# Attention followed by a gated unit on one core: the first queries in two halves, bfloat16 constants, 37 weight steps on GpSimd, a new order of work for block 0

## The chip, the cores and the metric

The kernel runs on one core of a Trainium2 chip. A core has five engines with queues of their own, which run beside each other and meet through semaphores: TensorE (PE, its weight loads shown as PEld), VectorE (DVE), ScalarE (ACT), GpSimd (POOL) and SyncE (SP), whose queue issues nearly all DMAs. The metric is the device time of one execution in microseconds (us).

## The reference

Eight batches (called blocks here) of 576 tokens pass through attention with eight heads of 64 columns; four heads see a local window of 32 keys, four see every 32nd key. What comes out, 4608 tokens of 512 columns, goes through a gated unit with 1536 hidden columns.

```python
scores = scale * np.matmul(q, k.transpose(0, 1, 3, 2))
mask_local = (rel >= 0) & (rel < 32)
mask_strided = (rel >= 0) & (pos[None, :] % 32 == pos[:, None] % 32)
scores = np.where(masks, scores, -1e9)
attn = np.exp(scores - np.max(scores, axis=-1, keepdims=True))
attn = attn / (np.sum(attn, axis=-1, keepdims=True) + 1e-09)
x = np.matmul(attn, v)            # heads side by side: 4608 x 512
gate = 1.0 / (1.0 + np.exp(-(x @ w_gate)))
out = (gate * (x @ w_val)) @ w_out
```

## The kernel before

**The large products.** Each float32 operand is split into a high and a low part that TensorE multiplies at its rate for rounded values, and a product is made of three matmuls (high by high, high by low, low by high; line 550 for gate and value, line 581 for the output). There are 12 slices f of the hidden columns; slice f needs three weights, f.0 (gate), f.1 (value), f.2 (output), and there are 36 in all. Later blocks are taken two at a time with a scheme of sums and differences (line 816).

**A weight's way.** A weight comes from memory as 64-bit words (`wr`, line 231, SP). ACT makes two words of it (`wa` line 252, `wb` line 256), DVE shifts one (`ws`, line 260) and adds the two as integers (`wd`, line 264, which DVE does with an instruction of its own on 16-bit halves), ACT rounds the sum to the high part (`wu`, line 268), and DVE subtracts that from the sum for the low part (`wl`, line 271). `whole` and `lower`, the functions behind `wd` and `wl`, already take the engine as an argument.

**Attention by pairs.** A block has four pairs of heads: 0 and 2 are local, 1 and 3 strided. For pair p of block b the steps are: loads `fQb.p` and `fVb.p`; scores `fS` (line 349, and for block 0 the mask, added by matmuls with a bfloat16 identity and mask, line 360); `fA` the row maximum (line 383), `fU` its subtraction (line 393), `fE` the exponential on ACT (line 408), `fN` the row sum (lines 412 to 414: sum, plus 1e-9, reciprocal), `fWp` the row multiplication on POOL (line 418; `fW` is the same on DVE); then a transposition, in block 0 on PE (`fT`, lines 426 and 430; ACT copies it out in `fP`, lines 447 and 449), later on DVE (`fB`, line 439); `fX` the product with v (line 471); and `fH` (ACT, line 507), `fL` (DVE, line 511) and `fR` (ACT, line 520), which split the result into the rows of x. In the text S0.3 is the score step of block 0, pair 3, and so for T, X, A, U and the others.

**Products of block 0.** As x of block 0 comes pair by pair, the products of the first slices are cut in four: `fgf.i.c` is the part of weight f.i with one 128-row chunk of x (three matmuls); `fgf.i` is a whole one (twelve). `of` is the output product of slice f (twelve); `s`, `m`, `x`, `y` are the sigmoid, the gating and the split of the hidden values.

**Order.** All steps are written out in one long list, `ORDER`; each engine does its share in the order of that list, and a DMA queue is an engine in this sense. Which PSUM bank a step uses is in `BANKS` (default `a`; X0.0 has o1, X0.1 o0, T0.0 and T0.1 share a, T0.2 o0). A step that uses a bank waits until what was there before has been read.

**Constants.** `cst` (float32: local mask, strided mask, identity; line 871) and `half` (bfloat16, the strided mask repeated; line 874) are two loads.

**The end.** `glu_out` for the last group makes the four row tiles in the order 0, 2, 1, 3. `give_out` (line 597) copies a finished tile from PSUM and stores it with two DMAs (line 603); tile 3 is copied in two halves of columns, first by ACT, then by DVE, and each engine's half is stored with two DMAs by one queue, ACT's by ACT and DVE's by SP.

Of the kernel before, what the change touches and what calls it, by code (L numbers as in the profile page):

```python
# [20 lines left out]
DM, DF = 512, 1536  # L21
# [41 lines left out]
    "X0.0": "o1", "S0.1": "o1", "X0.1": "o0", "S0.2": "o0", "T0.2": "o0", "X0.2": "o0", "S0.3": "o1", "T0.3": "o0", "X0.3": "o1", "g1": "a",  # L63
# [12 lines left out]
fQ0.0 fZ0.1 fZ0.3 K fQ0.1 C fQ0.2 fV0.1 fQ0.3 wr0.1 wr0.0 fV0.0 fV0.3 fV0.2 fS0.0 wr1.1 wr1.0 wr0.2 fS0.1 fA0.0 fQ1.0 wr2.0 wr2.1 fU0.0 wr1.2 fE0.0  # L76
fA0.1 fS0.2 fN0.0 fU0.1 fWp0.0 fA0.2 fE0.1 fS0.3 fU0.2 fN0.1 fE0.2 fT0.0 wb0.1 fN0.2 fWp0.1 fP0.0 wb0.0 fA0.3 wa0.1 fWp0.2 fT0.1 fU0.3 wa0.0 wr3.0
wr2.2 ws0.1 fX0.0 fP0.1 wd0.1 fE0.3 ws0.0 fX0.1 fN0.3 fH0.0 fV1.0 fR0.0 wu0.1 wd0.0 fWp0.3 fH0.1 fR0.1 fL0.1 wu0.0 wa1.1 fL0.0 fT0.2 wb1.1 wl0.0 wb1.0
wr3.2 ws1.1 fg0.0.0 wd1.1 fP0.2 wl0.1 wu1.1 fg0.0.1 wa1.0 wl1.1 fT0.3 wa0.2 wr3.1 ws1.0 wb0.2 wd1.0 fg0.1.0 fP0.3 ws0.2 wr4.0 fS1.0 wd0.2 wu1.0 wl1.0
wu0.2 fX0.2 wa2.0 fM1.0 fQ1.1 wb2.0 ws2.0 fA1.0 wr4.1 fX0.3 fH0.2 wa2.1 fL0.2 fR0.2 wd2.0 fg1.0.0 fH0.3 ws2.1 wu2.0 fg0.1.1 fL0.3 wb2.1 fg0.0.2 wl2.0  # L80
wa1.2 wr4.2 fg0.1.2 fU1.0 wb1.2 fg1.1.0 wd2.1 wr5.0 fE1.0 fg0.0.3 ws1.2 wu2.1 fN1.0 fg1.0.1 fg1.1.1 wl2.1 fg1.0.2 s0.0 fW1.0 wa2.2 fg1.1.2 wd1.2 wb3.0
fg0.1.3 wl0.2 wu1.2 fg2.0.0 m0.0 fR0.3 fg1.1.3 fB1.0.0 x0.0 fg2.0.1 wa3.1 y0.0 wa3.0 fg2.1.0 wl1.2 wb3.1 fg1.0.3 wr5.2 fB1.0.2 wr6.0 o0.0 s0.1 wa4.0
m0.1 fB1.0.1 x0.1 wb4.0 y0.1 wb2.2 fg2.1.1 wr6.2 ws3.0 wa4.1 wr5.1 fS1.1 fB1.0.3 wb3.2 wb4.1 wd3.0 fZ1.1 fg2.0.2 fQ1.2 fM1.1 wu3.0 wr7.0 fg2.1.2 wa3.2
# [36 lines left out]
c3.0.1.6 y3.0 V3.0.5 e2.3 B12.3 d2.3 G3.0.7 r8 B12.0 V3.0.7 Z13 c3.0.0.7 ad3.0.0.7 G3.0.4 c3.0.1.7 sg3.0.7 ad3.0.1.7 V3.0.4 sg3.0.4 mu3.0.7 G3.0.3 r9  # L120
# [54 lines left out]
y8.11 ob8  # L175
"""
FEW, MOST = slice(0, BY_PE), slice(BY_PE, B)
NEG = -1.0e30
SCALE = 1.0 / D**0.5


@with_exitstack
def attention_then_glu(ctx, tc, qk_l, qk_s, v_l, v_s, w_all, consts, halves, out):
# [689 lines left out]
    def half_constants():  # L873
        nc.sync.dma_start(half, halves)
# [124 lines left out]
```

## Time and profile before

| | us |
|---|---|
| median of three runs | 936.56 |
| the three runs | 935.67, 936.56, 936.94 |
| the profiled execution | 936.08 |
| its span, first to last instruction | 934.2 |
| PE busy | 916.7 (98%) |
| PE weight loads | 755.3 (81%) |
| DVE busy | 614.2 (66%) |
| ACT busy | 428.7 (46%) |
| POOL busy | 125.9 (13%) |

The profile is of one execution. Times in its rows count from the start of the span. A timeline row gives the start, the duration, the engine, the line, the operation, the tiles written and read, and in brackets the idle time of the engine before it and what ended that. A row of a group gives the total, then the mean in ns, then the idle time before. Matmuls are pipelined, so the duration of one is longer than the distance to the next.

### The profile page before, as it was taken

What the parts mean: (1) busy time and instruction counts of PE and PEld (TensorE: products, weight loads), DVE (VectorE), ACT (ScalarE), POOL (GpSimd) and SP (SyncE); (2) the same over time, 40 slices, a digit from 0 to 9 for tenths busy, and PEclk for the clock granted to TensorE, in tenths of its full rate; (3) what the DMA queues carried; (4) which work ended last, traced back from release to release, by engine and by line L of the source; (5) the groups of instructions that cost most, each with busy time, mean ns of one, the idle gap of its engine ahead of it and who ended that gap; (6) DMA issues with size and microseconds to landing.
All of it is one profiled execution on the core that took longest, in us unless ns stands there. A gap on an engine that the chain in (4) does not pass through costs nothing.

```text
span 934.2 us, 18488 instructions
## 1 busy us (share of the span) xinstructions
PE 916.7 (98%) x7608; PEld 755.3 (81%) x7608; DVE 614.2 (66%) x1013; ACT 428.7 (46%) x775; POOL 125.9 (13%) x186
## 2 busy tenths in 40 slices
PE   6799999999999999999999999999999999999998
PEld 4688888888888888888888888888888888888886
DVE  5799996667689989766667897766347343333331
ACT  3789764334455455444445444444435233332231
POOL 2000003545415623000000120000003000000000
PEclk9999999999999999999999999999999999999999
DMA  9862535554556675656555425654444055444111
GB/s 352 307 230 89 185 96 174 176 175 154 179 190 190 216 222 199 215 191 188 173 190 177 149 99 175 207 189 143 145 141 144 12 168 187 143 156 140 64 45 46
DMA packets 90212, 154.60 MB, mean 166 GB/s; under 512 B 5904, under 2 KB 40336, under 8 KB 90128
## 3 DMA queue, kind: packets, MB, share of 16 engines
q1 hardware_dynamic: 89648, 152.77, 50.4%
q8 instruction: 60, 0.98, 0.4%
q10 hardware_dynamic: 480, 0.66, 0.3%
q14 instruction: 24, 0.20, 0.1%
HBM read 121.94 MB, written 31.46 MB: 164 GB/s over the span
## 4 chain that ended last, share of the span: by engine, by line
PE 98%; DMA 1%; issue 0%; DVE 0%; ACT 0%; SPq 0%
PE o L581 22%; PE p L816 21%; PE d L816 16%; PE g L550 10%; PE v L550 10%; PE o_a L581 5%; PE o_g L581 3%; PE o_v L581 3%; PE x_a L471 2%; PE x L471 1%; PE s_v L349 1%; PE s_g L349 1%; PE s L349 1%; DMA qk<-in_qk_s 1%; PE gv L550 1%; PE t L426 1%
## 5 line engine op out<-in xcount | busy, mean ns | idle before, releaser
L816 PE MATMUL p<-xs,ring 128*128 128x512 f32 x864 | 204.6, 389 | 0.0
L816 PEld LDWEIGHTS p<-xs,ring 128*128 128x128 f32 x864 | 162.2, 188 | 33.6
L581 PE MATMUL o<-w,hh 128*128 128x512 f32 x576 | 180.7, 395 | 0.0
L816 PE MATMUL d<-xs,ring 128*128 128x512 f32 x648 | 155.7, 389 | 0.0
L816 PEld LDWEIGHTS d<-xs,ring 128*128 128x128 f32 x648 | 121.7, 188 | 25.2
L581 PEld LDWEIGHTS o<-w,hh 128*128 128x128 f32 x576 | 106.1, 188 | 22.7
L439 DVE STREAM_TRANSPOSE pt<-sb 32x320 f32<-32x320 f32 (+1 forms) x224 | 120.0, 536 | 4.2
L581 PE MATMUL o<-w,hl 128*128 128x512 f32 x288 | 112.1, 389 | 0.0
L850 DVE TENSOR_TENSOR e<-e,d 128x512 f32<-128x512 f32 x54 | 37.1, 688 | 108.1 <-PE d L816 62.1
L550 PE MATMUL g<-xh,w 128*128 128x512 f32 x256 | 86.3, 395 | 0.0
L550 PE MATMUL v<-xh,w 128*128 128x512 f32 x256 | 85.8, 392 | 0.0
L845 ACT COPY e<-p 128x512 f32<-128x512 f32 x54 | 31.8, 588 | 116.6 <-PE p L816 116.4
L581 PEld LDWEIGHTS o<-w,hl 128*128 128x128 f32 x288 | 54.1, 188 | 11.5
L550 PEld LDWEIGHTS g<-xh,w 128*128 128x128 f32 x256 | 48.7, 190 | 10.5 <-issue 0.2
L550 PEld LDWEIGHTS v<-xh,w 128*128 128x128 f32 x256 | 48.5, 189 | 10.1
L744 POOL TENSOR_TENSOR sum<-sum 128x128 f32<-128x128 f32 x96 | 51.9, 543 | 6.5
L574 DVE TENSOR_TENSOR hl<-hid,hh 128x512 fp32r<-128x512 f32 x36 | 28.0, 780 | 34.0 <-ACT hh L570 33.8
L550 PE MATMUL g<-xl,w 128*128 128x512 f32 x128 | 50.3, 393 | 0.0
L550 PE MATMUL v<-xl,w 128*128 128x512 f32 x128 | 50.1, 391 | 0.0
L739 POOL TENSOR_TENSOR sum<-w 128x256 f32<-128x256 f32 x44 | 34.7, 809 | 98.8 <-DMA sets<-sum 71.3
L858 ACT ACTIVATE e<-e 128x512 f32<-128x512 f32 x54 | 34.2, 634 | 27.9 <-DVE e L850 27.6
L570 ACT CAST hh<-hid 128x512 fp32r<-128x512 f32 x36 | 22.5, 624 | 49.5 <-PE o_a L581 41.1
(149 smaller groups left out, 1373.7 us busy)
## 6 DMA issues: line engine op xcount, KB each, us to landing
ring<-sets SPq DMA_DIRECT2D x126, 512.0 KB, 4.1
raw<-in_w_all SPq DMA_DIRECT2D x36, 512.0 KB, 4.7
vv<-in_v_l SPq DMA_DIRECT2D x15, 640.0 KB, 4.8
qk<-in_qk_l SPq DMA_DIRECT2D x15, 608.0 KB, 5.6
qk<-in_qk_s SPq DMA_DIRECT2D x15, 599.0 KB, 5.9
out<-ob SPq DMA_DIRECT2D x32, 256.0 KB, 2.1
sets<-w SPq DMA_DIRECT2D x24, 256.0 KB, 3.4
sets<-sumh SPq DMA_DIRECT2D x24, 256.0 KB, 2.9
```

The lines of the kernel that those rows point to most:

```text
L349: nc.tensor.matmul(sc[j % len(sc)][g * m : (g + 1) * m, j // len(sc) * BANK + s * kk : j // len(sc) * BANK + (s + 1) * kk], q[d], k[d], st ...
L439: nc.vector.transpose(dst[to : to + LB, :, col : col + LB], src[part * LB : (part + 1) * LB, :, h * LB : (h + 1) * LB])
L471: nc.tensor.matmul(at_bank(r, (u * per + g) * m, (u * per + g + 1) * m)[j * D : (j + 1) * D], v[part][rows, slot * P + j * D : slot * P + ...
L550: nc.tensor.matmul(o, w, x, start=first and n == 0, stop=last and n == len(todo) - 1)
L574: by.tensor_tensor(hl, whole_h.pop((k, f)), hh.bitcast(F32), op=ALU.subtract)
L581: nc.tensor.matmul(acc[k][i], h[:, i * P : (i + 1) * P], w, start=f == 0 and n == 0, stop=f == NF - 1 and n == 2,)
L739: nc.gpsimd.tensor_tensor(u[:, at : at + 2], part(wh[f][i], c), part(wl[f][i], c), op=ALU.add)
L744: nc.gpsimd.tensor_tensor(u[:, to], u[:, x], u[:, y], op=op)
L816: nc.tensor.matmul(to, w[:, (wi * 2 + c) * P : (wi * 2 + c + 1) * P], x[xi][:, c], start=p in (1, 2, 5) and c == j == 0, stop=c == 1 and j ...
L845: nc.scalar.copy(x, two[m, 0])
L850: nc.vector.tensor_tensor(x, x, two[m, 1], op=ALU.add)
L858: nc.scalar.activation(x, x, AF.Sigmoid)
```

## The change

- The first load (`fQ0.0`, 128 x 1216 float32) becomes two, `fQa0.0` and `fQb0.0`, each with the queries and keys of one half of the tokens; the scores of pair 0 become `fSa0.0` and `fS0.0`, 40 matmul pieces each, the second with the mask.
- The float32 constants and the longer bfloat16 ones are replaced by one bfloat16 load (`K`), 128 x 502; the strided mask is read repeatedly by its access pattern, and a float32 identity is made from it by a copy on POOL (`C`).
- For the strided pairs the 1e-9 stands in a padding column beside the probabilities, and the row sum takes it in; the separate addition goes.
- 23 of the integer adds (`wd` becomes `wdp`) and 14 of the subtractions (`wl` becomes `wlp`) are done by POOL, 37 in all; three more row multiplications of block 1 go there too (`fW` becomes `fWp`).
- The list is new for block 0: among others the order of loads (V after queries and the first two weights), U0.1 before N0.0, S0.3 before S0.2, T0.1 and X0.1 before T0.0 and X0.0, and groups of the first products between X0.2 and X0.3. Banks change with it. From block 1 on the list has the same steps on PE in the same order, with small moves elsewhere.
- The last row tile is copied whole by ACT, and its two stores are issued one by ACT's queue and one by SP's.

```diff
 BANKS = {
-    "X0.0": "o1", "S0.1": "o1", "X0.1": "o0", "S0.2": "o0", "T0.2": "o0", "X0.2": "o0", "S0.3": "o1", "T0.3": "o0", "X0.3": "o1", "g1": "a",
+    "S0.0": "o0", "T0.0": "o0", "S0.1": "o1", "T0.1": "o1", "X0.1": "o1", "S0.2": "o0", "T0.2": "o0", "X0.2": "o1", "S0.3": "o1", "X0.3": "o0",
+    "S1.0": "o0", "X1.0": "o0", "g1": "a",
 }
...
-fQ0.0 fZ0.1 fZ0.3 K fQ0.1 C fQ0.2 fV0.1 fQ0.3 wr0.1 wr0.0 fV0.0 fV0.3 fV0.2 fS0.0 wr1.1 wr1.0 wr0.2 fS0.1 fA0.0
-fQ1.0 wr2.0 wr2.1 fU0.0 wr1.2 fE0.0 fA0.1 fS0.2 fN0.0 fU0.1 fWp0.0 fA0.2 fE0.1 fS0.3 fU0.2 fN0.1 fE0.2 fT0.0 wb0.1 fN0.2
-fWp0.1 fP0.0 wb0.0 fA0.3 wa0.1 fWp0.2 fT0.1 fU0.3 wa0.0 wr3.0 wr2.2 ws0.1 fX0.0 fP0.1 wd0.1 fE0.3 ws0.0 fX0.1 fN0.3 fH0.0
-fV1.0 fR0.0 wu0.1 wd0.0 fWp0.3 fH0.1 fR0.1 fL0.1 wu0.0 wa1.1 fL0.0 fT0.2 wb1.1 wl0.0 wb1.0 wr3.2 ws1.1 fg0.0.0 wd1.1 fP0.2
-wl0.1 wu1.1 fg0.0.1 wa1.0 wl1.1 fT0.3 wa0.2 wr3.1 ws1.0 wb0.2 wd1.0 fg0.1.0 fP0.3 ws0.2 wr4.0 fS1.0 wd0.2 wu1.0 wl1.0 wu0.2
-fX0.2 wa2.0 fM1.0 fQ1.1 wb2.0 ws2.0 fA1.0 wr4.1 fX0.3 fH0.2
+fQa0.0 fZ0.1 fZ0.3 K fQb0.0 fQ0.1 fQ0.2 fQ0.3 wr0.1 wr0.0 fV0.1 fSa0.0 fV0.2 C fV0.0 fS0.0 wr1.1 wr1.0 fV0.3 fA0.0
+fQ1.0 wr2.0 fS0.1 wr2.1 fU0.0 wr0.2 wr1.2 fE0.0 fA0.1 fU0.1 fN0.0 fE0.1 fS0.3 fN0.1 wb0.1 wa0.1 fS0.2 fA0.3 fWp0.1 wr3.0
+wb0.0 fU0.3 wa0.0 fWp0.0 fA0.2 fT0.1 fE0.3 wr2.2 fU0.2 fP0.1 ws0.0 fT0.0 ws0.1 wdp0.0 fE0.2 fN0.2 fX0.1 fP0.0 wdp0.1 wu0.0
+fN0.3 fX0.0 fH0.1 fWp0.2 fR0.1 fL0.1 wu0.1 fH0.0 fV1.0 wl0.1 fWp0.3 fT0.2 fR0.0 wa1.1 fL0.0 wb1.0 ws1.1 fg0.1.0 fP0.2 wb1.1
+fT0.3 wl0.0 wa1.0 wd1.1 wr3.2 wr3.1 ws1.0 fg0.0.0 wu1.1 wdp1.0 fP0.3 fS1.0 wl1.1 wu1.0 fX0.2 fQ1.1 fM1.0 wa2.0 wlp1.0 wb2.0
+fA1.0 fg1.1.0 fH0.2 wr4.1 ws2.0 wb2.1 fg0.0.1 fL0.2 wdp2.0 wa2.1 fg1.0.0 fU1.0 fR0.2 wr4.2 wb0.2 fg1.1.1 wu2.0 fX0.3 ws2.1
...
-    cst = pool.tile([P, SL * KL + GS + P], F32, name="cst")
+    cst = pool.tile([P, 64 * -(-(SL * KL + GS + P) // 64)], BF16, name="cst")[:, : SL * KL + GS + P]
+    ident = pool.tile([P, P], F32, name="ident")
...
-                nc.gpsimd.memset(sb[:, : 2 * ns * QB].rearrange("p (t k) -> p t k", k=QB)[:, :, GS:], 0.0)
+                pad = sb[:, : 2 * ns * QB].rearrange("p (t k) -> p t k", k=QB)[:, :, GS:]
+                nc.gpsimd.memset(pad[:, :, :1], TINY)
+                nc.gpsimd.memset(pad[:, :, 1:], 0.0)
...
-                seen = half[:, : ns * kk] if local else half[:, SL * KL : SL * KL + ns * kk]
+                seen = cst[:, : ns * kk] if local else mask_s.broadcast_to([P, ns, kk])
...
-            nc.vector.tensor_reduce(row, prob, axis=AX.X, op=ALU.add)
-            nc.vector.tensor_scalar_add(row, row, 1e-9)
+            if local:
+                nc.vector.tensor_reduce(row, prob, axis=AX.X, op=ALU.add)
+                nc.vector.tensor_scalar_add(row, row, TINY)
+            else:
+                prob = tiles["sb"][:, : 2 * ns * QB].rearrange("p (t k) -> p t k", k=QB)[:, :, : kk + 1]
+                nc.vector.tensor_reduce(row, prob, axis=AX.X, op=ALU.add)
...
-        queue = nc.scalar if by == nc.scalar.copy else nc.sync
         for n in range(P // REST):
             at = (i * P // REST + n) * S + TB
+            queue = (nc.scalar, nc.sync)[n if i == NTT - 1 else int(by != nc.scalar.copy)]
             queue.dma_start(out[at : at + REST, cut], ob[n * REST : (n + 1) * REST, cut])
...
-            give_out(k, NTT - 1, slice(0, DM // 2), nc.scalar.copy)
-            give_out(k, NTT - 1, slice(DM // 2, DM), nc.vector.tensor_copy)
+            give_out(k, NTT - 1, by=nc.scalar.copy)
```

More of the change, by code (lines that the diff above doesn't have):

```diff
@@ L80 @@
[L80 to L83, printed above, removed]
@@ L176 @@
+sg7.5.7 ad7.5.1.7 V7.5.4 sg7.5.4 mu7.5.7 G7.5.3 mu7.5.4 x7.11 V7.5.3 y7.11 ad7.5.0.3 o7.9 ad7.5.1.3 sg7.5.3 mu7.5.3 o7.10 x8.0 y8.0 o7.11 x8.1 e7.0
+y8.1 d7.0 e7.1 d7.1 o8.0 x8.2 y8.2 e7.2 d7.2 o8.1 e7.3 x8.3 d7.3 y8.3 o8.2 x8.4 y8.4 o8.3 x8.5 y8.5 o8.4 x8.6 y8.6 o8.5 x8.7 y8.7 o8.6 x8.8 y8.8 o8.7
+x8.9 y8.9 o8.8 x8.10 y8.10 o8.9 x8.11 y8.11 ob8
 """
@@ L178, with attention_then_glu @@
 NEG = -1.0e30
+TINY = 1e-9
 SCALE = 1.0 / D**0.5
 @with_exitstack
-def attention_then_glu(ctx, tc, qk_l, qk_s, v_l, v_s, w_all, consts, halves, out):
+def attention_then_glu(ctx, tc, qk_l, qk_s, v_l, v_s, w_all, consts, out):
     nc = tc.nc
@@ L186, in attention_then_glu @@
     work = ctx.enter_context(tc.tile_pool(name="work", bufs=1))
-    cst = pool.tile([P, SL * KL + GS + P], F32, name="cst")
+    cst = pool.tile([P, 64 * -(-(SL * KL + GS + P) // 64)], BF16, name="cst")[:, : SL * KL + GS + P]
+    ident = pool.tile([P, P], F32, name="ident")
     mask_l = cst[:, : SL * KL].rearrange("p (j n) -> p j n", j=1)
     mask_s = cst[:, SL * KL : SL * KL + GS].rearrange("p (t k) -> p t k", t=1)
-    ident = cst[:, SL * KL + GS :]
     mxs = pool.tile([P, 64], F32, name="mxs")
@@ L357, in score @@
             if b == 0 and part != 0:
-                seen = half[:, : ns * kk] if local else half[:, SL * KL : SL * KL + ns * kk]
+                seen = cst[:, : ns * kk] if local else mask_s.broadcast_to([P, ns, kk])
                 for j in range(2):
-                    nc.tensor.matmul(
-                        sc[0][:, j * BANK : j * BANK + ns * kk], half[:, -P:], seen, start=False, stop=True, skip_group_check=True
-                    )
+                    to = sc[0][:, j * BANK : j * BANK + ns * kk]
+                    if not local:
+                        to = to.rearrange("p (t k) -> p t k", k=kk)
+                    nc.tensor.matmul(to, cst[:, -P:], seen, start=False, stop=True, skip_group_check=True)
             todo["soft"] = [x.rearrange("p (j n) -> p j n", n=BANK)[:, :, : ns * kk] for x in sc]
@@ L629, in attention_then_glu @@
     first = first_area.enter_context(tc.tile_pool(name="first", bufs=1))
-    half = first.tile([P, SL * KL + SS * GS + P], BF16, name="half")
     x_tiles(0)
@@ L871, in constants, with whole_ident @@
         nc.sync.dma_start(cst, consts)
-    def half_constants():
-        nc.sync.dma_start(half, halves)
+    def whole_ident():
+        nc.gpsimd.tensor_copy(ident, cst[:, SL * KL + GS :])
     STEPS = dict(
-        C=constants, K=half_constants, fQ=first_steps("Q"), fQa=lambda b, p: firsts[b, p]["Q"](0), fQb=lambda b, p: firsts[b, p]["Q"](1),
+        K=constants, C=whole_ident, fQ=first_steps("Q"), fQa=lambda b, p: firsts[b, p]["Q"](0), fQb=lambda b, p: firsts[b, p]["Q"](1),
         fSa=lambda b, p: in_parts(b, p, 0), fB=lambda b, p, j: firsts[b, p]["B"](j), fV=first_steps("V"), fZ=first_steps("Z"), fM=first_steps("F"), fA=first_steps("A"), fU=first_steps("U"),
@@ L974, in _layouts @@
         [np.where(mask_l.reshape(P, -1), 0.0, NEG), np.where(mask_s, 0.0, NEG), np.eye(P)], 1
-    ).astype(np.float32)
-    halves = np.concatenate(
-        [np.where(mask_l.reshape(P, -1), 0.0, NEG), np.tile(np.where(mask_s, 0.0, NEG), (1, SS)), np.eye(P)], 1
     ).astype(ml_dtypes.bfloat16)
-    return [np.ascontiguousarray(a) for a in (qk_l, qk_s, v_l, v_s, w_all, consts, halves)]
+    return [np.ascontiguousarray(a) for a in (qk_l, qk_s, v_l, v_s, w_all, consts)]
 def kernel(q, k, v, moe_w_gate, moe_w_val, moe_w_out):
```

195 lines of the change are left out of this document (98 added, 97 removed).

## The prediction

> **What bounds the kernel now.** I read the page first, then the busy times by stretch.
>
> ```profile
> span 934.2 us, 18488 instructions
> ...
> q8 instruction: 60, 0.98, 0.4%
> ```
>
> ```profile
> 0.00:40.00 40.00, 26.86 (x614) 21.11 (x615) 25.00 (x48) 21.82 (x47) 5.86 (x10) 0.97 0.93 358
> 40.00:140.00 100.00, 100.00 (x810) 81.66 (x810) 95.64 (x179) 78.59 (x138) 0.68 (x2) 0.99 0.47 151
> ...
> 900.00:934.20 34.20, 29.81 (x132) 24.37 (x130) 7.41 (x12) 6.88 (x12) 0.00 (x0) 0.97 0.16 46
> ```
>
> The columns are PE, PEld, DVE, ACT, POOL, clock, DMA share, GB/s. PE idles 13.1 us in the first 40 us, 4.4 us in the last stretch, and never between 40 and 140. So the time can only change at the head and the tail, unless a new wait opens in the middle, where DVE is the engine without slack (95.6 of 100 us). The timeline of PE shows where the head's idle time lies; a bracket is the idle time before a row and what ended it.
>
> ```profile
> 5.29 1.41 PE L349 MATMUL s<-qk 64*32 64x64 f32 x80 [5.29 <-DMA qk<-in_qk_l]
> 6.62 0.72 PE L360 MATMUL s<-half 128*128 128x320 bf16 x2
> 8.08 1.55 PE L349 MATMUL s<-qk 64*64 64x54 f32 x48 [0.74 <-DMA qk<-in_qk_s]
> ...
> 13.13 0.48 PE L349 MATMUL s<-k,q 64*64 64x54 f32 x8 [0.86 <-DVE sb L393]
> 14.12 1.33 PE L349 MATMUL s<-k,q 64*64 64x54 f32 x40 [0.52 <-issue]
> ...
> 18.18 1.51 PE L426 MATMUL t<-cst,sb 128*128 128x128 f32 x6 [0.88 <-ACT pt L449]
> 19.62 3.80 PE L471 MATMUL x<-pt,vv 64*64 64x32 f32 x116
> 25.46 1.08 PE L426 MATMUL t<-cst,sb 128*128 128x128 f32 x4 [2.03 <-DVE xl L511]
> ...
> 31.64 1.04 PE L349 MATMUL s<-qk 64*32 64x64 f32 x80
> ...
> 37.58 0.41 PE L471 MATMUL x<-pt,v 54*64 54x54 f32 x7 [2.83 <-issue]
> 37.92 0.79 PE L550 MATMUL gv<-xh,w 128*128 128x512 f32 x1
> ...
> 41.33 0.39 PE L550 MATMUL g<-xh,w 128*128 128x512 f32 x1
> ```
>
> The row at 25.46 waits for DVE because the third transpose (T0.2) shares PSUM bank o0 with X0.1, which DVE must have read. The stall of 2.83 us lies inside a run of tiny matmuls and waits for no engine. I take it for instruction fetch: 0.98 MB in 60 packets for 2x7608 instructions of PE is 64 bytes each and about 256 a packet. PE's two "issue" stalls come after 222 matmuls with their weight loads (444) and after 602 (1204): 760 apart, three blocks. Block 4 began 61 matmuls into S1.0, at 31.64 + 0.74 = 32.4, and block 5 was there at 37.58: 5.1 us for a fetch beside a DMA system 93% busy. After the stall the eight 128x512 matmuls from 37.92 to 41.33 take 3.41 us; later, by the chain that ended last, twelve take 2.72:
>
> ```profile
> 43.77 2.72 PE gv L550 x12
> ...
> 138.38 2.94 PE v L550 x12
> ```
>
> So the idle PE came back at a lower rate, and eight matmuls that should take 1.8 us lost 1.6 us more.
>
> **Part by part: the first load.** By the DMA view:
>
> ```profile
> qk<-in_qk_l SPq DMA_DIRECT2D x1, 608.0 KB, 4.5
> qk<-in_qk_s SPq DMA_DIRECT2D x1, 599.0 KB, 6.4
> ```
>
> The first landed at 0.74 + 4.5 = 5.28, the second at 1.65 + 6.4 = 8.04; with the 193 KB of the mask between them that is 792 KB in 2.8 us, 283 KB/us. Now 304 KB land first, then 126 KB of constants, then the other 304 KB. The second half has 126 KB more ahead of it: 5.28 + 0.44 = 5.72. By then the first 40 matmuls are done; the other 40 take 0.67 (half of 6.62 - 5.29), the mask 0.72: scores finished at 7.1 instead of 7.34. The halving alone is worth 0.2 us. Ahead of the end of qk of pair 1 lie 1332 KB instead of 1400: 0.24 us earlier, 7.84, and its scores end 2.2 us later (1.55 and the mask, overlapping), 10.04.
>
> **The head's new list.** DVE now subtracts pair 1's maximum (bank o1) before it sums pair 0, and S0.3 runs before S0.2.
>
> ```profile
> 7.38 0.82 DVE L383 TENSOR_REDUCE mx<-s 128x10 f32<-128x640 f32 x1 [7.38 <-PE s L360]
> 8.24 0.82 DVE L393 TENSOR_TENSOR sb<-s,mx 128x640 f32<-128x640 f32 x1
> ...
> 28.36 0.69 DVE L271 TENSOR_TENSOR w<-words,w 128x512 fp32r<-128x512 f32 x1
> ...
> 38.78 0.82 DVE L511 TENSOR_TENSOR xl<-x,xh 128x288 fp32r<-128x288 f32 x3 [2.29 <-ACT xh L507]
> ...
> 47.28 0.69 DVE L563 TENSOR_TENSOR t<-e,v 128x512 f32<-128x512 f32 x1 [1.71 <-PE v L550]
> ...
> 70.07 1.30 DVE L271 TENSOR_TENSOR w<-high,w 128x512 fp32r<-128x512 f32 x2
> ...
> 136.92 0.69 DVE L271 TENSOR_TENSOR l<-high,h 128x512 fp32r<-128x512 f32 x1
> ```
>
> Maximum and subtraction take 0.82 each: o1 is free at 11.7. S0.3 (same shape as S0.1, 2.2 us) ends 13.9, S0.2 (same shape as S0.0, 2.05 us) 15.95. T0.1 (1.5 us) follows at once in o1, which U0.3 leaves at 15.5. T0.0 needs o0 free of S0.2: 15.95 + 1.64 = 17.6, ends 19.1. X0.1 and X0.0, 3.8 us together, end 22.9. X0.0 now has bank a and X0.1 has o1, so T0.2 in o0 waits for neither: 22.9 instead of 25.46, 2.5 us earlier. The V loads go behind 1.3 MB of queries and weights; at the 358 GB/s of the first 40 us the 3.95 MB up to pair 1's V are there at 14.6 and the 5.2 MB up to pair 0's at 18.2, before 19.1 and 20.6. If that cover failed, X would wait by the difference.
>
> POOL, which had the four row multiplications of block 0 already, now has two integer adds ahead of those of pairs 2 and 3. It can begin them when DVE has shifted the first weight, near 18.4; at 1.29 us a step (row below) pair 2 is done at 22.3 and pair 3 at 23.6, before T0.2 at 22.9 and T0.3 near 25.5.
>
> **The fetch and the rate.** Four groups of three matmuls (0.68 each) now lie between X0.2 and X0.3. The block border, 1204, falls 28 matmuls into X0.3: 0.2 of S1.0, 1.3 of X0.2, 2.7 of groups and 0.5 make 4.7 us since the border before, against 5.1: a stall of 0.4 instead of 2.83. That saves 2.4 us, and with no long gap the 1.6 us of slow matmuls. Lead: 2.5 + 2.4 + 1.6 = 6.5 us. (The Trainium skill, "Runtime: NRT & Kernel Launch", section "Instruction fetch mechanics", also has blocks of 256 instructions, but calls the cost of a border mostly hidden; the 2.83 us here say otherwise. By that page the stall would have another cause and stay, and the sum would be that of rival 2.)
>
> **Can DVE follow?** PE's lead is worth only what the weights allow. Weight 11.1 is split at 136.92 and done at 137.61; PE begins with it at 138.38, so DVE had 0.8 us to spare. 6.5 us earlier means 131.9. DVE now: from 28.36 (weight 1.1, which cannot come much sooner, as its words follow X0.0 on ACT) to 136.92 are 108.6 us. 35 weight steps leave it, 0.60 us each (two take 1.30, and the last 0.69 overlaps by 0.09 with what follows), and 3 multiplications of 0.82, the size of the subtraction: -23.5; the two waits of 2.29 and 1.71 us, which PE's stall and lateness caused, -4.0. What comes back is the wait for POOL:
>
> ```profile
> 348.56 1.29 POOL L790 TENSOR_TENSOR xd<-xraw,xraw 128x512 f32<-128x512 f32 x1 [7.48 <-DVE mx L413]
> ...
> 348.85 1.69 DVE L418 TENSOR_TENSOR sb<-sb,mx 128x648 f32<-128x648 f32 x1
> ```
>
> ```profile
> L850 DVE TENSOR_TENSOR e<-e,d 128x512 f32<-128x512 f32 x54 | 37.1, 688 | 108.1 <-PE d L816 62.1 <-ACT e L845 45.8
> ...
> L574 DVE TENSOR_TENSOR hl<-hid,hh 128x512 fp32r<-128x512 f32 x36 | 28.0, 780 | 34.0 <-ACT hh L570 33.8
> ...
> L802 DVE TENSOR_TENSOR xs<-xd,xs 128x512 fp32r<-128x512 f32 x24 | 21.5, 907 | 0.0
> ...
> L802 DVE TENSOR_TENSOR xs<-xraw,xs 128x512 fp32r<-128x512 f32 x18 | 13.9, 790 | 7.9 <-ACT xs L798 7.9
> ```
>
> The first pair: POOL's step holds DVE's, which ends 0.69 after POOL's end, 0.69 after 349.85. DVE groups with two SBUF inputs near POOL's 18 steps of L790 are stretched over 688 ns by 36x92, 24x219 and 18x102 ns, 10.4 us, 0.6 us for each POOL step. (The Trainium skill, "SBUF — State Buffer", section "Who interferes with whom", says the same as a lock: a DVE instruction with two SBUF inputs and a GpSimd one that reads SBUF exclude each other for a whole instruction. It speaks against this change; the trace agrees, by the 1.69 us.) With 37 POOL steps after 28.36: +22. Bounds for one: nothing, where DVE happens to reduce or transpose, to 0.86 or 1.0, where it is caught at once. I take 0.6, from the nearest like work. Sum: 28.4 + 108.6 - 23.5 - 4.0 + 22.2 + 0.7 = 132.4, 0.5 late against 131.9. PE keeps 6.0 us. POOL's integer add has no row: I take 1.29 us, between DVE's 0.69 and twice 1.29; 40 such steps fill about 52 of POOL's 110 us. The last bound would make 82 us, still inside, but with more for DVE to wait on. After 140 both lists hold the same PE work, and DVE has slack.
>
> **The tail.**
>
> ```profile
> 927.63 0.59 ACT L597 COPY ob<-o_a 128x512 f32<-128x512 f32 x1 [1.26 <-PE o_a L581]
> ...
> 929.85 0.37 ACT L597 COPY ob<-o_a 128x256 f32<-128x256 f32 x1 [1.64 <-PE o_a L581]
> ...
> 930.71 1.11 SPq L603 DMA_DIRECT2D out<-ob  x2
> ```
>
> ```profile
> out<-ob ACTq DMA_DIRECT2D x2, 128.0 KB, 2.3
> ...
> out<-ob SPq DMA_DIRECT2D x2, 64.0 KB, 2.1
> ```
>
> Now the last of SP's two stores is issued at 931.2 and lands 2.1 later, 933.3. One copy of 0.59 ends at 930.44, and each queue issues one store at 930.46; 128 KB land 2.3 later, 932.8. That saves 0.5 (0.2 to 0.8; SP is free by 930.4, just in time). Pad memsets, the 126 instead of 251 + 193 KB, and the copy of the identity lie beside other work.
>
> **Sum.** 6.0 + 0.5 = 6.5 us off the profiled execution's 936.08, which is 0.5 below the median of 936.56: 930.1 against that median.
>
> **Rivals.** 1, slower: POOL blocks DVE, and DVE becomes the bound. The point of change is where all 6.5 + 0.5 are lost: 0.5 us late by 22.2 us of waits, so 28.7 us, 0.78 per POOL step. For it: 95.6% busy, and most DVE steps there have two SBUF inputs. Against it: transposes, reductions and PSUM readers do not wait. At 0.86 per step, 31.8 us: 132.4 + 9.6 = 142.0, 10.1 late: 936.56 + 10.1 - 6.5 - 0.5 = 939.7. 2: the stall stays at 2.83 with its slow matmuls (fetch counted wrongly, or T0.2 late by POOL): lead 2.5, which DVE can follow; with the tail 936.56 - 3.0 = 933.6. 3, no change to be measured: waits near 0.78 per step eat the lead, or the list's early half stalls on its own weights: about 936.5. That the halved load brings its matmuls forward but not its mask is already in the sum.
>
> **How the numbers follow.** A measurement here tells 0.2%, 1.9 us, from no change. Forecast 0.53 (928 to 932.5), rival 2 0.20, rival 3 0.09, rival 1 0.18 (937 to 945). Faster takes the first two and a little of the third: 0.74; same 0.08; slower 0.18. The range, 927.5 to 938.0, takes in the forecast with a lead better by 2.5 us (DVE unhindered, a faster first group) and the nearer third of rival 1.
>
> **What would show it.** T0.2 near 23 with no wait for xl; the "issue" gap under 1 us; matmul groups at 0.68 by 35; DVE steps of L264, L271 or L418 at 1.2 to 1.8 us beside POOL; PE busy in 40 to 140 with at most 1 us of gaps, these near weights 10 and 11; the two last stores starting together. Gaps of PE ahead of the products of weights 3.0 to 5.0, or a POOL add well over 1.6 us, would prove me wrong.

## The result and the profile after

On one chip, six executions of each kernel: before 936.61 us (935.25 to 937.56), after 930.13 us (928.07 to 931.07). The ratio is 0.9929, with a 95% interval of 0.9919 to 0.994: 6.5 us faster. The profiled execution of the changed kernel took 930.32 us with a span of 928.3; before it was 936.08 and 934.2.

The windows view of the changed kernel shows where PE still waits. Its columns are the stretch, then the busy time of PE, PEld, DVE, ACT and POOL, then the granted clock, the DMA share and GB/s.

```profile
0.00:40.00 40.00, 29.72 (x637) 22.59 (x638) 28.23 (x46) 25.02 (x54) 14.93 (x21) 0.91 0.96 366
40.00:140.00 100.00, 100.00 (x813) 81.55 (x812) 87.67 (x141) 76.50 (x136) 52.42 (x46) 1.00 0.51 166
```

From 40 to 140 PE never idles, although it gets there earlier, and DVE is busy for 87.7 of the 100 us. All that is left to wait for lies in the head, 10.28 us (40 - 29.72), and behind the last matmul. The longest waits of PE in the changed kernel (us in total, how many, the longest of them):

```profile
PE s L353 <- DMA qk<-in_qk_l: 4.7, 2, 3.7
PE s L353 <- DVE sb L398: 1.8, 1, 1.8
PE v L560 <- DVE xl L521: 1.0, 1, 1.0
PE t L436 <- POOL sb L428: 0.9, 1, 0.9
...
PE x L481 <- issue: 0.4, 1, 0.4
```

The "issue" stall of 2.83 us and the transpose that waited 2.03 us for the low part have gone. In their place stand a subtraction of pair 1 (1.8), a low part that the first product wants (1.0) and a row multiplication on POOL (0.9). PE's timeline of the changed kernel, around the same steps as the lines shown of before:

```profile
18.63 1.55 PE L481 MATMUL x<-pt,vv 54*64 54x54 f32 x72
20.62 0.97 PE L481 MATMUL x<-pt,vv 64*64 64x32 f32 x44 [0.43 <-issue]
22.48 0.66 PE L436 MATMUL t<-ident,sb 128*128 128x128 f32 x4 [0.89 <-POOL sb L428]
...
24.86 0.79 PE L560 MATMUL v<-xl,w 128*128 128x512 f32 x1 [1.01 <-DVE xl L521]
...
28.57 1.41 PE L353 MATMUL s<-qk 64*32 64x64 f32 x80
...
34.48 1.21 PE L481 MATMUL x<-pt,v 54*64 54x54 f32 x44
35.62 0.50 PE L560 MATMUL v<-xh,w 128*128 128x512 f32 x1
```

T0.2 starts at 22.48 instead of 25.46, 2.98 us earlier. X0.3 at 34.48 runs its 44 matmuls in one go. At 35.62 PE has 18 of the large matmuls (128x512) behind it, six ahead of S1.0 and twelve behind X0.2. Before, nine lay ahead of S1.0, and with the nine behind X0.3 the same point is reached at 41.56:

```profile
41.56 0.40 PE L550 MATMUL v<-xh,w 128*128 128x512 f32 x1
```

So the lead is 5.94 us. It is made of 2.98 at T0.2, 2.83 for the stall and 1.6 for the slow matmuls behind it. Off that go 1.01 for the new wait at 24.86 and 0.67 because S1.0 and X0.2 now run in a slow stretch (28.57 to 31.53 is 2.96, before 31.64 to 33.93 was 2.29); 0.2 is left over. From there to the end nearly all of it is kept. By the chain of work that ended last, weight 11.1 is used at

```profile
132.94 2.72 PE v L560 x12
```

against 138.38, 5.4 us earlier. The last matmul ends at 924.08 against 929.82, 5.7 us earlier, and the span is 5.9 us shorter.

### The profile page after: what moved, and what is told of

It is laid out like the page before. It is cut to its first block, busy times and chain, and to the rows that moved or that the text cites. A ratio compares the mean times of both kernels' runs of the same rounds, so it can differ in the third digit from the quotient of the medians.

```text
span 928.3 us, 18510 instructions
## 1 busy us (share of the span) xinstructions
PE 913.8 (98%) x7608; PEld 751.8 (81%) x7608; DVE 602.7 (65%) x956; ACT 427.4 (46%) x775; POOL 180.4 (19%) x243
## 4 chain that ended last, share of the span: by engine, by line
PE 98%; DVE 1%; DMA 1%; ACT 0%; SPq 0%; issue 0%
PE o L591 22%; PE p L824 21%; PE d L824 16%; PE v L560 10%; PE g L560 10%; PE o_a L591 5%; PE o_g L591 3%; PE o_v L591 3%; PE x_a L481 2%; PE s L353 1%; PE s_g L353 1%; PE s_v L353 1%; PE x L481 1%; PE gv L560 1%; DMA qk<-in_qk_s 1%; PE t L436 0%
## 5 line engine op out<-in xcount | busy, mean ns | idle before, releaser
L747 POOL TENSOR_TENSOR sum<-w 128x256 f32<-128x256 f32 x44 | 32.6, 760 | 84.7 <-DMA sets<-sum 60.7
```

The costliest lines, as they stand in the source:

```text
L747: nc.gpsimd.tensor_tensor(u[:, at : at + 2], part(wh[f][i], c), part(wl[f][i], c), op=ALU.add)
```

## The experiments

Each kernel ran beside the kernel before on the same chip; ratios are to that. The list is `ORDER`; where only names of steps in it move or change, the diff shows those names.

### GpSimd: how many steps, and what each costs

**All steps back on VectorE, in the new list.**

```diff
-wdp0.0 ... wlp11.0 (37 steps)   fWp1.0 fWp1.2 fWp1.3
+wd0.0  ... wl11.0               fW1.0  fW1.2  fW1.3
```

> The changed kernel with the 37 weight steps and the three row multiplications of block 1 back on VectorE, the list otherwise the same. By the sum of the prediction, with the waits for GpSimd as the changed kernel's trace shows them (14 us in all instead of 22): VectorE gets 23.5 us more work and loses 14 us of waits; weight 11.1, ready at 129.4, would be ready at 134 to 139 against 132.9 when it is wanted, so TensorE waits in the middle, and the time is 931.5 to 936.5, most likely 933.5. Rival: the steps on GpSimd are not needed, the list alone brings the gain, and the head's two waits for GpSimd (0.9 and 1.0 us) go too: 928.5 to 930.

Measured: 935.89 us, ratio 0.9991 (0.9981 to 1.0). The new list without the GpSimd steps is worth 0.2% at most. The longest of PE's waits from 46 to 200 us in this kernel:

```profile
PE o L591 <- ACT hh L580: 1.7, 1, 1.7
PE x L481 <- DVE pt L449: 0.8, 1, 0.8
```

There are none in this stretch in the kernel before or in the changed one. ACT, for whose `hh` PE waits longest, had waited for DVE in its turn:

```profile
132.94 0.62 ACT L580 CAST hh<-t 128x512 fp32r<-128x512 f32 x1 [4.72 <-DVE t L573]
```

So with the lead VectorE cannot follow. From 46 to 140 PE loses 3.3 us (busy 53.28 of 54 and 37.46 of 40), and the granted clock from 100 to 140 is 0.96; the twelve matmuls behind the wait of 1.7 take 4.56 us instead of 2.94. This kernel has X0.3 behind it at 34.88, 6.7 us ahead of the kernel before at the same count of large matmuls; it uses weight 11.1 at 138.17, only 0.2 us ahead.

**Every second step back on VectorE.**

```diff
-wdp0.0 wdp1.0 wdp2.0 wdp0.2 wlp3.0 ... (19 of 37)
+wd0.0  wd1.0  wd2.0  wd0.2  wl3.0  ...
```

> The changed kernel with every second of its 37 weight steps on GpSimd put back on VectorE, 19 of them; the order stays. Theory (each step takes 0.635 us off VectorE and costs it 0.38 us of waiting, so gains 0.25; VectorE had 3.6 us to spare at weight 11.1): 19 x 0.25 = 4.8 us, of which 3.6 were to spare, so 1.2 us late: 931.3, between 930 and 932.5. Rival (VectorE has no use for the spare time, since single steps come late long before 11.1): 932.5 to 933.5, half of the way to the 935.9 of all steps on VectorE. Second rival (the prediction's 0.6 us per step): putting back 19 costs 0.6 us, 930.7.

Measured: 930.51 us, ratio 0.9932 (0.9918 to 0.9946); the changed kernel beside it on that chip 930.66, 0.9933 (0.992 to 0.9945). So half of the steps are as good as all, to within these intervals. The time lies inside the theory's range and on the second rival's figure; the price decides between them, and the first line under part 1 of the page (busy time, share, instructions) gives it. First the kernel with no weight step on GpSimd, then with half of them, then the changed kernel's repeat (the last run below):

```profile
PE 915.7 (98%) x7608; PEld 752.7 (81%) x7608; DVE 610.6 (65%) x996; ACT 426.8 (46%) x775; POOL 125.8 (13%) x203
```

```profile
PE 913.6 (98%) x7608; PEld 751.4 (81%) x7608; DVE 605.6 (65%) x975; ACT 426.8 (46%) x775; POOL 154.7 (17%) x224
```

```profile
PE 914.0 (98%) x7608; PEld 752.1 (81%) x7608; DVE 601.5 (65%) x956; ACT 427.6 (46%) x775; POOL 181.1 (19%) x243
```

From none to all, 37 steps of 0.60 and three multiplications of 0.82 us leave DVE, 24.7 us by the prediction's durations, and its busy time falls by 9.1. So 15.6 us came back as stretched DVE steps: 0.39 for each of the 40. From half to all it is 19 x 0.60 = 11.4 against 4.1, so 7.3 us, 0.38 each. DVE's busy time differs between executions of the changed kernel: the two others with a trace have 602.7 and 600.5, which makes it 0.36 to 0.42 from none to all and 0.33 to 0.45 from half to all. So the price is about 0.4, where the prediction took 0.6. With half of the steps, PE loses 0.42 us in 46 to 140, to one wait of `o` for ACT's `hh`, which had itself waited 4.74 us for DVE: VectorE is close to being the bound there.

**The same steps on GpSimd in the kernel before, with the list of before.**

```diff
-wd0.0 ... wl11.0   fW1.0 fW1.2 fW1.3   (in the list of before)
+wdp0.0 ... wlp11.0 fWp1.0 fWp1.2 fWp1.3
```

> The kernel before with its own list, but with the same 37 weight steps and three row multiplications on GpSimd. Theory: TensorE never waited between 40 and 140 us, so relief of VectorE alone brings nothing; the stall and the wait for X0.1 stay, and the first weights come up to 1.5 us later because an add takes 1.3 us instead of 0.7: 936.6 to 938. Rival: the steps on GpSimd bring the gain by themselves: 931 to 933.

Measured: 944.13 us, ratio 1.0088 (1.0071 to 1.0105): 7.7 us slower, which no theory had. DVE's busy time did fall, from 614.2 to 608.7, by 5.5 of the 24.7 us, so here a step cost DVE 0.48. But PE now waits; the longest rows of its waits from 46 to 200 us in this kernel (its line numbers are about a hundred lower, as the list was written in fewer lines):

```profile
PE g L451 <- POOL w L172: 2.0, 1, 2.0
PE x L372 <- DVE pt L340: 1.6, 1, 1.6
PE v L451 <- POOL w L172: 1.1, 1, 1.1
```

In that stretch PE idles 7.5 us in all (windows view: busy 51.98 of 54, 36.13 of 40, 58.40 of 60). Of these 7.5 us, 3.1 end with a weight's step on POOL; the rest end with DVE's steps or ACT's, and how far POOL had held those up was not separated. A weight's step that takes 0.69 us on DVE takes about 1.4 on POOL. In the old list the last step of the gate weights of slices 4 to 8 stands 0 to 2 of PE's steps ahead of the product that uses it, in the new list 2 to 7. That is the likely reason why the steps pay only in the new list; it was not tried by itself.

### The stall in X0.3

Two kernels were to shift the borders of the instruction blocks with empty instructions ahead of all else, 176 in the kernel before and 126 in the changed one.

```diff
     with tc.manual_schedule():
+        for _ in range(176):
+            nc.tensor.nop(nofuse=True)
```

> The kernel before with 176 empty instructions at the start of TensorE's queue, where it waits 5.3 us for its first data anyway; nothing else. Fetch theory: the borders of the 256-instruction blocks move back by 176 instructions, from 444, 1204 to 268, 524, 780, 1028 (counted in matmuls and weight loads), and none is left in the burst S1.0, X0.2, X0.3 that follows another border by less than 5 us; the stall of 2.83 us at 34.75 is gone and the products after it run at 0.68 us a group; the time falls by 3.3 to 4.4 us, to 932.2 to 933.3, limited by VectorE's 0.8 us of slack and the 4.0 us of its waits that go. Rival (the stall has another cause, such as the V load or a semaphore): it stays within X0.3, 936.6.

> The changed kernel with 126 empty instructions at the start of TensorE's queue. Fetch theory: one block border falls on the first pieces of S1.0 and the next near the 49th matmul of X0.2, 2.4 us later, so a stall of about 2.7 us appears inside X0.2, where there was none, and slow matmuls behind it: 930.1 + 2.7 to 4.3 = 932.8 to 934.4. Rival: no stall, 930.1.

Measured: 936.02 us, 0.9995 (0.9986 to 1.0005), and 929.27 us, 0.9915 (0.9899 to 0.9932). Neither tells anything of the theory, since the borders did not move. The kernel before with 176 empty instructions, X0.3 and the instruction queue:

```profile
32.93 0.82 PE L471 MATMUL x<-pt,v 54*64 54x54 f32 x37
37.14 0.47 PE L471 MATMUL x<-pt,v 54*64 54x54 f32 x7 [3.40 <-issue]
```

```profile
q8 instruction: 60, 0.98, 0.4%
```

The stall comes after the same 37 matmuls as without them, the queue brought the same 60 packets, and the page counts the same 18488 instructions. By these signs what was added never reached the stream that PE reads, and these two runs are repeats of the two kernels. As a repeat the second is of use: here the border of the changed kernel does show.

```profile
33.91 0.67 PE L481 MATMUL x<-pt,v 54*64 54x54 f32 x28
35.32 0.45 PE L481 MATMUL x<-pt,v 54*64 54x54 f32 x16 [0.74 <-issue]
```

It lies 28 matmuls into X0.3, where the prediction's count of 1204 had put it, with 0.74 us instead of the 0.4 worked out.

**X0.3 ahead of the four groups again.** This moves real instructions.

```diff
-fX0.2 fQ1.1 ... wu2.0 fX0.3 ws2.1
+fX0.2 fX0.3 fQ1.1 ... wu2.0 ws2.1
```

> The changed kernel with one step of its list moved: X0.3 stands directly behind X0.2, as in the kernel before, so that its 44 small matmuls come ahead of the four groups of three 128x512 matmuls (2.7 us) instead of behind them. Nothing else changes. Theory (the stall is the arrival of the next block of instructions): the border then lies 40 matmuls into X0.3 (28 where X0.3 stood, and 12 more for the 24 instructions that no longer precede it), and PE stands still there for 2.4 to 3.2 us with no engine to wait for; the matmuls behind it may run at 0.63 instead of 0.39 us for a while. Time 932.5 to 934.9. Rival (the stall of 2.83 us had another cause, which the new list removed or which comes and goes by itself): no stall at matmul 40, time 929.0 to 930.8.

Measured: 934.3 us, ratio 0.9969 (0.9955 to 0.9983), 3.6 us more than the changed kernel beside it. The six times lie in two groups of three, about 3 us apart, and the median between them. PE's timeline of one of the longer executions:

```profile
31.71 0.88 PE L481 MATMUL x<-pt,v 54*64 54x54 f32 x40
35.30 0.47 PE L481 MATMUL x<-pt,v 54*64 54x54 f32 x4 [2.70 <-issue]
35.70 0.80 PE L560 MATMUL gv<-xh,w 128*128 128x512 f32 x1
...
40.98 0.47 PE L560 MATMUL v<-xh,w 128*128 128x512 f32 x1
```

The stall is back, 2.70 us within the 2.4 to 3.2, and after 40 matmuls, not 28 or 37: it stays at its place in the count of instructions while the work around it moves. Behind it the four groups take 5.28 us (35.70 to 40.98) instead of 2.72. The rival falls.

The DMA view of a short window shows when a packet of instructions was under way: the line of its queue has the number of packets that start in the window, MB, and the time of these packets as a share of 16 engines. For the kernel before, 35.00 to 35.10, and the kernel with X0.3 early, 32.90 to 33.00:

```profile
q8 instruction: 1, 0.02, 68.1%
```

```profile
q8 instruction: 1, 0.02, 67.5%
```

68.1% of 16 x 0.1 us is 1.09 us, 67.5% is 1.08. So a packet was there near 36.1 and PE went on at 37.58, 1.4 us later; in the other kernel near 34.0 and 35.30, 1.3 us later. In all the traces, each "issue" stall of PE in the first 40 us ends 1.2 to 1.6 us behind the end of such a packet. This is what PE waits for. In the changed kernel the same packet starts at 32.84, and with 1.07 us and as much again as elsewhere the instructions are there by 35.1 to 35.5; PE reaches the border near 35.2, and no stall shows.

### The banks, the load and the tail, each alone in the kernel before

```diff
-"X0.0": "o1", "S0.1": "o1", "X0.1": "o0", "S0.2": "o0", ...
+"S0.1": "o1", "X0.1": "o1", "S0.2": "o0", ...
```

> The kernel before with two PSUM banks changed: X0.0 in bank a and X0.1 in o1, so that T0.2 in o0 does not wait until X0.1 is read. Theory: T0.2 begins at 23.5 instead of 25.46, but the first product then waits for its weight's low part, 26.5 instead of 27.8, so 1.3 us of the 2.0 come through and the fetch stall stays: 935.3. Rival: VectorE has no slack to let the lead through, 936.6.

Measured: 937.04 us, ratio 1.0008 (0.9998 to 1.0017), no gain. PE's timeline:

```profile
21.17 3.80 PE L471 MATMUL x<-pt,vv 64*64 64x32 f32 x116 [0.95 <-ACT pt L447]
24.90 1.11 PE L426 MATMUL t<-cst,sb 128*128 128x128 f32 x4
...
37.88 0.47 PE L471 MATMUL x<-pt,v 54*64 54x54 f32 x6 [3.15 <-issue]
```

T0.2 no longer waits for the low part, but X0.0 in bank a waits 0.95 us for the copy of the transposes there, and X starts at 21.17 instead of 19.62. T0.2 comes 0.56 us earlier, not 2. That is spent on two small waits of the first product and a longer stall: X0.3 goes on at 37.88, before at 37.58. The banks need the list that frees a in time.

```diff
-fQ0.0 fZ0.1 fZ0.3 K fQ0.1 C
+fQa0.0 fZ0.1 fZ0.3 K fQb0.0 fSa0.0 fQ0.1 C
```

> The kernel before with the first load in two halves alone and pair 0's scores in two parts. Theory: first matmul near 3.7 instead of 5.3, but the first row maximum only at 7.2 instead of 7.38, because the second half stands behind the mask's load; 936.4. Rival: the maximum follows the first matmul and starts 1 us earlier or more.

One execution, 937.64 us; the difference in time is not resolved. PE's timeline:

```profile
3.55 0.94 PE L349 MATMUL s<-qk 64*32 64x64 f32 x44 [3.55 <-DMA qk<-in_qk_l]
7.20 0.87 PE L349 MATMUL s<-qk 64*32 64x64 f32 x36 [2.71 <-DMA qk<-in_qk_l]
```

The first matmul is early, as expected, but the second half, issued at 1.64 behind the mask's 193 KB, is there only at 7.20, and the first maximum starts at 8.76 instead of 7.38 (in other traces with the first loads of before, 6.62 to 6.69). In the changed kernel, with 125.5 KB of constants between the halves, it is there at 5.65. The 68 KB more are worth 0.24 us at the prediction's 283 KB per us and do not explain 1.55; the rest is open. In this execution the halving without the smaller constants made the head worse.

```diff
-queue = nc.scalar if by == nc.scalar.copy else nc.sync
+queue = (nc.scalar, nc.sync)[n if i == NTT - 1 else int(by != nc.scalar.copy)]
...
-give_out(k, NTT - 1, slice(0, DM // 2), nc.scalar.copy)
-give_out(k, NTT - 1, slice(DM // 2, DM), nc.vector.tensor_copy)
+give_out(k, NTT - 1, by=nc.scalar.copy)
```

> The kernel before with the new end alone: last row tile copied whole by ScalarE, its two stores from two queues. Theory: from the end of the last matmul to the end of the span 3.8 to 3.9 us instead of 4.3, the last store issued at about 0.65 us after the last matmul's end instead of 1.4; about 936.1. Rival: the landing of 128 KB instead of 64 KB takes the gain back, 4.3 us.

One execution, 936.56 us; the trace tells more than the time. The last copy and store on ACT's queue in this kernel:

```profile
930.51 0.58 ACT L597 COPY ob<-o_a 128x512 f32<-128x512 f32 x1 [1.63 <-PE o_a L581]
931.13 0.50 ACTq L603 DMA_DIRECT2D out<-ob  x1
```

The last matmul ends at 930.48 and the span at 934.7, 4.2 us later; before it was 929.82 to 934.2, 4.4. The changed kernel has 924.08 to 928.3, 4.2 as well. The tail is worth 0.2 us, by one trace of each kernel.

### A version that may be better

The wait of 1.01 us at 24.86 comes from one subtraction ahead of the low part in DVE's list. The rows of DVE and POOL in the changed kernel:

```profile
21.90 0.75 DVE L521 TENSOR_TENSOR xl<-x,xh 128x288 fp32r<-128x288 f32 x3
22.57 1.64 DVE L273 TENSOR_TENSOR w<-high,w 128x512 fp32r<-128x512 f32 x1
24.13 0.68 DVE L521 TENSOR_TENSOR xl<-x,xh 128x512 fp32r<-128x512 f32 x1
```

```profile
21.16 2.50 POOL L428 TENSOR_TENSOR sb<-sb,mxs 128x640 f32<-128x640 f32 x2 [0.42 <-DVE mxs L424]
```

The subtraction of L273, 0.69 us elsewhere, lasts until 24.21, 0.55 us beyond the end of POOL's multiplications at 23.66. Two kernels move it behind the low part; the second also moves X0.3 one group later. The third is the changed kernel as it is.

```diff
-fV1.0 wl0.1 fWp0.3 fT0.2 fR0.0 wa1.1 fL0.0 wb1.0
+fV1.0 fWp0.3 fT0.2 fR0.0 wa1.1 fL0.0 wl0.1 wb1.0
...                                   (second kernel only)
-wu2.0 fX0.3 ws2.1 ... fg0.1.1 fH0.3
+wu2.0 ws2.1 ... fg0.1.1 fX0.3 fH0.3
```

> The changed kernel with one step moved: VectorE splits pair 0's result (L0.0) before the low part of weight 0.1, which waits for GpSimd. If the lock between VectorE and GpSimd is what delays the second matmul of the first group by 1.0 us, that wait falls to about 0.5 us and the time to about 929.6; if the slow matmul rate between 25 and 31.5 us comes from this gap, up to 2 us more is gained, 927.5. Rival: no effect, 930.1.

> The changed kernel with two steps of its list moved: the low part of weight 0.1 behind the low part of X0.0, and X0.3 one group of three matmuls (0.68 us) later. Theory: the wait of 1.01 us for the low part of X0.0 goes, and the border of the instruction blocks in X0.3 (0.65 and 0.74 us in two runs) is covered by the group: 1.0 to 1.7 us less than the changed kernel as it stands beside it, 928.4 to 929.1 where that is 930.1. Rival (the lead is eaten by VectorE later): as the changed kernel.

> The changed kernel as it is, once more, for the run beside it. Both theories: 929.0 to 930.8; in the trace a stall of 0 to 0.8 us after 28 matmuls of X0.3, by when the run reaches them.

Measured: 929.17 us, 0.9917 (0.9903 to 0.9932), for the first; 928.81 us, 0.9918 (0.9905 to 0.9932), for the second; 930.66 us, 0.9933 (0.992 to 0.9945), for the changed kernel on the chip of the second. The wait for the low part is gone in both traces and the span of the first is 926.4. The medians say 1.8 us less than the changed kernel beside it, but the intervals overlap, and the repeat of the changed kernel with empty instructions had 929.27 on the chip of the first. A gain of this size is likely and not shown. The second kernel's profiled execution, its slowest of four with 930.61, has something else to show:

```profile
17.80 1.81 PE L499 MATMUL x<-pt,vv 54*64 54x54 f32 x72
22.89 1.57 PE L499 MATMUL x<-pt,vv 64*64 64x32 f32 x44 [3.28 <-issue]
```

That is the border one block earlier, after 72 matmuls of X. It cost 0.43 us in the changed kernel's profile, nothing in its two repeats, and 3.28 here. The packet of instructions that starts at 18.09 in the changed kernel starts at 20.55 here; why it came late is open. X0.3, one group later, shows no stall here.

## Why the prediction was right

**The first load: the landing right, the gain by luck.** The second half landed at 5.65 (5.72 worked out; by the trace it feeds 36 of the 80 pieces, not 40). The first maximum starts at 7.20, 0.18 us earlier than in the profile before (0.2), and pair 1's scores are done at 9.97 (10.04). But the profile before was an odd one here. Four other traces with the same first loads (176 empty instructions, GpSimd steps, banks, tail) have the first data at 4.53 to 4.60 instead of 5.29, and the first maximum at 6.62 to 6.69. The first row is of the kernel with the new tail, the second of the changed kernel:

```profile
6.62 0.82 DVE L383 TENSOR_REDUCE mx<-s 128x10 f32<-128x640 f32 x1 [6.62 <-PE s L360]
```

```profile
7.20 0.82 DVE L388 TENSOR_REDUCE mx<-s 128x10 f32<-128x640 f32 x1 [7.20 <-PE s L367]
```

The kernels with the changed loads have 7.14 to 7.63, so against those four the first maximum came later, not earlier. What may have gained is pair 1: its maximum starts at 9.63 to 10.55, against 10.29 to 10.83 with the loads of before. The early first maximum of those four was of no use either: the kernel with the new tail starts S1.0 at 31.68, the kernel before at 31.64.

**The new list and the banks: right, with one wait missed.** T0.2 came 2.98 us earlier, 2.5 forecast, because TensorE had its full rate back by then in this execution: X ran from 18.63 to 21.59, 2.96 us with a stall of 0.43, instead of 3.8. The cover that the prediction named, POOL's row multiplications, did not hide quite all: T0.2 waited 0.9 us for one. The wait of 1.01 us for the low part of X0.0 was not foreseen. It is POOL holding a DVE step, which the prediction had priced, at a place where PE was close behind. The prediction asked what POOL costs as a total over 110 us and not at single steps with no slack. Neither wait appears where X is slower. In the repeat with empty instructions X ran at the lower rate:

```profile
19.31 3.76 PE L481 MATMUL x<-pt,vv 54*64 54x54 f32 x116
23.00 1.11 PE L436 MATMUL t<-ident,sb 128*128 128x128 f32 x4
```

There T0.2 came at 23.00, as forecast, without a wait for POOL, and the low part was not waited for either. S1.0 started at 28.57 in both executions. So what the full rate gave ahead of it, the waits for POOL and DVE took back.

**The fetch: right.** The stall sat where 1204 instructions had put it, and four groups ahead of it covered it but for 0 to 0.74 us (0 in the profile and in the last repeat, 0.74 in the repeat with empty instructions, 0.45 with half of the steps on GpSimd). Putting X0.3 back brought back 2.70 us of stall and the slow matmuls, and 3.6 us of time by the median; the prediction had 4.0 for both. That the stall hangs on the count of instructions is shown by that, and that PE waits for a packet of instructions by the times of the packets. The time from border to border, 5.1 us by the prediction, is 5.5 with X0.3 early (the border before lies 64 matmuls into S1.0, near 29.8, and PE goes on at 35.30). It is not fixed. In the kernel before with empty instructions, banks, halves or tail it is 5.6 to 5.9, with stalls of 3.15 to 3.56; with the GpSimd steps the packet started soon after the border before it and the stall was 1.40. Only about 1.1 us of it is the packet's transfer. In the profiled changed kernel the slow S1.0 and X0.2 left the packet more time, so by this account part of the 0.67 us that they cost was won back at the border. The Trainium skill, "Runtime: NRT & Kernel Launch", section "Instruction fetch mechanics", has blocks of 256 instructions, refilled while the engine works, and calls the cost of a border mostly hidden. The blocks agree with the counts here. The cost is hidden in these traces after 40 us, where PE has no "issue" stall, and not among the hundreds of tiny matmuls of the first 40 us, with the DMA share at 0.93 to 0.97: there one cost 3.40 in the rows above.

**Can DVE follow: right, by two wrong terms that partly cancel.** The step said 0.6 us of waiting per POOL step, 22.2 us, weight 11.1 ready at 132.4 and 0.5 late. The runs give about 0.4 per step. In the changed kernel:

```profile
128.67 0.69 DVE L273 TENSOR_TENSOR l<-high,h 128x512 fp32r<-128x512 f32 x1
```

The low part is ready at 129.36 and wanted at 132.94: 3.6 us to spare instead of 0.5 late. With 0.38 for the price the prediction's sum would give 124.3, 5.1 us too early. The other wrong term is DVE's idle time. From 28.4 to 136.9 DVE was idle for 7.1 us before (busy 101.41 of 108.5), and the sum took 4.0 of that away; in the changed kernel it is idle for 7.9 us from 28.4 to 129.4 (busy 93.10 of 101), 4.8 more than the 3.1 that the sum leaves. It waits now for PE's products and for ACT.

The 0.6 came from a stretch where DVE's steps beside POOL's were mostly of two SBUF inputs; in blocks 0 and 1 reductions, transposes and steps that read PSUM lie between them. Between 28 and 137 us these keep their mean durations (transposes 569 and 502 ns before, 569 and 503 after; the gating of L573, which reads PSUM, 686 and 683), while the low parts of L273 go from 687 to 943 ns and the shifts of L262, which take a scalar, from 426 to 561. The mix is the likely reason for the lower price and was not tried by itself. The Trainium skill, "SBUF — State Buffer", section "Who interferes with whom", excepts reductions and steps with one SBUF input, and says that an operation with a scalar may all the same take the port shared with GpSimd. The trace agrees with the last point too: besides the shifts, one step of 0.17 us elsewhere took 1.20 while POOL added integers, as DVE's timeline of the changed kernel has it:

```profile
19.57 1.20 DVE L420 TENSOR_SCALAR mxs<-mxs 128x10 f32<-128x10 f32 x1
```

POOL's own steps were a little dearer than forecast: its adds took 1.37 to 1.45 us on average between 20 and 140 us, 1.29 forecast. Rival 1 needed 0.78 per step and was far off. Rival 1's other face, that a POOL step comes late rather than that it holds DVE, was not in the prediction; in the kernel before with POOL steps, 3.1 of PE's 7.5 us of waits are of this kind.

**The tail: right in sign, mis-sized.** 0.5 was forecast and 0.2 came. The step took the landing of the last store as 2.3 us for 128 KB against 2.1 for 64. The DMA view of the changed kernel has 2.4 (ACT's queue) and 2.5 (SP's). Of the 0.5 worked out that takes 0.1 to 0.2; where the rest went was not tried.

**The sum.** The forecast lead of 6.5, of which 6.0 were to be kept, was 5.94 and 5.7: T0.2 and the stall gave 0.9 more than forecast, the new wait and the slow stretch took 1.7. That the sum came out at 930.1 owes something to these errors cancelling. Of the lead, the place of X0.3 was tried by itself in the new list (3.6 us); the earlier T0.2 was not. Half of the 37 steps on GpSimd would have done the same.

## What to carry to other kernels

A gain on one engine is worth what the next one can follow: here everything but the GpSimd steps gave 0.2% at most, those steps alone lost 0.9%, and together they gave 0.7%. Price an engine's interference twice, as a total against the slack of the whole stretch and as a single late step wherever the consumer is close behind. When tiny matmuls come in hundreds, count instructions to the next border and put large ones ahead of it.

## What the hardware showed that was not expected

The granted clock of a window can read 1.00 while TensorE runs at half its rate. In the kernel before, the stretch from 25.5 to 31.5 us reads 1.00, but the matmuls of the first product in it start 0.43 us apart, against 0.23 from 41.33 on:

```profile
25.50:31.50 6.00, 6.00 (x21) 4.54 (x21) 5.39 (x10) 4.71 (x10) 0.00 (x0) 1.00 1.02 410
```

```profile
27.41 0.63 PE L550 MATMUL g<-xl,w 128*128 128x512 f32 x1
27.84 1.05 PE L550 MATMUL g<-xh,w 128*128 128x512 f32 x2
```

So durations, not that column, tell the rate in the first 30 us. In the changed kernel the rate is full by 17.85 (four transposes take 0.63, before 1.08), slow again from 24.86, and full from 31.5. The executions of one kernel also differ in this: the kernel with X0.3 early has three times from 932.55 to 933.04 us with a clock of 0.996 and three from 935.55 to 935.87 with 0.992, and the one profiled, with twelve matmuls at half rate, took 935.55. That the three shorter ones had fewer matmuls at half rate would fit; they have no trace.
